# One token list for the order of attention on all engines, k and q evacuated apart, loads by single batches with q first

## The chip, the cores and the metric

The kernel runs on one core of a Trainium2 chip. The metric is the device time of one execution in microseconds (us), as the median of several runs. Each engine of the core (TensorE or PE for matrix products, VectorE or DVE, ScalarE or ACT, GpSimd or POOL, SyncE or SP) works off its own instructions in the order in which the program lists them; semaphores make one wait for another. DMAs that GpSimd, SyncE and ScalarE issue share 16 DMA engines.

## The reference

Two parts, the second fed by the first. Attention over 8 batches, 12 heads, 448 tokens and 64 features, with q and k normalised over the features:

```python
q_n, k_n = (rmsnorm(q, g_q), rmsnorm(k, g_k))      # x / sqrt(mean(x*x) + 1e-6) * g
scores = scale * np.matmul(q_n, k_n.transpose(0, 1, 3, 2))
attn = softmax(scores)
attn_out = np.matmul(attn, v)
```

Then a mixture of eight experts without a learned router. The output of attention, laid out as 3584 tokens by 768, is routed by a hash of each token's id, and a token goes through one expert only:

```python
expert_idx = token_ids * np.int64(2654435761) % np.int64(E)
for e in range(E):
    h = np.maximum(x[mask_e] @ w1[e], 0.0)          # 768 -> 1024
    out[mask_e] = h @ w2[e]                         # 1024 -> 768
```

## The kernel before

**Attention** goes by steps: a step is one pair of heads of one batch, so there are 48 steps, numbered 0 to 47, six to a batch. Steps are gathered in groups that are prepared together: groups 0, 1 and 2 hold the one, two and three head pairs of batch 0, every later group holds three (two groups to a batch, 17 groups in all).

*Preparation of a group*, for q (a = 0) and k (a = 1): `prep_sq` squares (VectorE, in a few cases ScalarE); `prep_sum` adds the squares by 16 products with the identity on TensorE; `prep_red` reduces them on VectorE; `prep_rr` makes the reciprocal root with Ln and Exp on ScalarE; `prep_norm` multiplies (four VectorE instructions); `prep_v` copies v (VectorE).

*A step*: `transposes` does eight transposes on TensorE (four for k, four for q) into one PSUM bank, `ps_qk`, of which there is one, used by the sums too. `transposed` evacuates them on VectorE, k with the gain to `kT`, then q to `qT`. `score` makes the scores in four pieces (TensorE), each into one of three `ps_sc` buffers, and ScalarE writes the exponential of each. `av_part` makes the products with v in three parts (TensorE, one `ps_av` buffer), and after the third part VectorE takes the reciprocal of the row sums and scales into `x_sb`. After a batch's sixth step `store_x` writes the batch to DRAM (SyncE).

The order is a loop over steps written out by hand: scores 1 and 2 of step s, transposes of s + 1 with their evacuation, score 3, two parts of the products of s - 1, score 0 of s + 1, then what three tables (`pre`, `mid`, `post`) hold for the preparation of later groups, with the third part of the products among it.

**Loads.** q, k and v come as float32 from DRAM and are cast to 16 bits on the way by DMAs that GpSimd issues, one after another in its program order (`load_q` two DMAs, `load_kv` four for k and four for v). Only step 0's q and k come by SyncE and ScalarE (float32). Buffers hold two batches each, two of every kind. Before the loop GpSimd issues batch 0 in two parts, batch 1 whole, batches 2 and 3 together; then it clears three gather buffers (L605), the pad slots of the second buffers, and makes constants (`setup2`, L115 to L139). Batches 4 and 5 are loaded together at step 7, 6 and 7 at step 19.

**Routing** (`p1` to `p11`, `table`, `table_mm`) works out which token goes to which slot of which expert. One piece is put into each step from step 14 on, behind that step's other work. Pieces use several engines: `p1` takes the low bits of the ids on VectorE and converts them on GpSimd (`eidf`, L367); `p2` compares on VectorE (`onehot`, L371) and converts the counts on GpSimd (`oc`, L374); `p3` multiplies them with `emask` and ones on TensorE (L382 to L384) and copies the products out on VectorE (`cmix`, L385):

```python
        def p2():
            V.tensor_tensor(out=onehot[:], in0=eidf[:, None, :].to_broadcast([P, E, NTC]), ...)
            V.reduce_sum(ot[:], onehot[:], axis=AX.X)
            G.tensor_copy(oc[:], ot[:])
```

**Experts.** From about step 44 GpSimd gathers tokens from DRAM; the first three tiles are transposed behind the last scores, then for each expert `gemm1` (L766), `gemm2` (L779) and an indirect store (L784). Weights of experts 0 and 1 are loaded during attention, the others afterwards, by GpSimd.

Of the kernel before, what the change touches and what calls it, by code (L numbers as in the profile page):

```python
# [19 lines left out]
def kernel(  # L20
# [12 lines left out]
    nc = tc.nc  # L33
# [70 lines left out]
    def setup():  # L104
        import dataclasses as _dc
        tid_t32 = _dc.replace(moe_token_ids.tensor, shape=[N * 2], dtype=I32)
        for base in (0, D):
            nc.sync.dma_start(out=gcol[base:base + D, 0:1], in_=g_q[:, None])
            nc.sync.dma_start(out=gcol[base:base + D, 1:2], in_=g_k[:, None])
        nc.scalar.dma_start(out=tid32[:],  # L110
                            in_=bass.AP(tensor=tid_t32, offset=0,
                                        ap=[[2 * NTC, P], [2, NTC], [1, 2]]))
# [86 lines left out]
    with tc.manual_schedule(), \  # L199
# [66 lines left out]
        def prep_sq(gi, a, on_act=False):  # L266
# [5 lines left out]
            if on_act:  # L272
# [4 lines left out]
        def prep_sum(gi, a, wide=False):  # L277
# [3 lines left out]
            if wide:  # L281
# [17 lines left out]


        def prep_rr(gi):
            n = groups[gi][2]
            ss = st[gi].pop("ss")
            m = 8 * n
            rr = a_st.tile([P, 2, GMAX * 8, 2], FP16, name="rr")
            nc.scalar.activation(ss[:, :, 0:m], ss[:, :, 0:m], AF.Ln, bias=eps_col[:], scale=1.0 / D)
# [3 lines left out]
            st[gi]["n8"] = a_n8.tile([P, 2, GMAX, 4, 2, D], FP16, name="n8")  # L310

        def prep_norm(gi):
            n = groups[gi][2]
            rr = st[gi].pop("rr")
            n8 = st[gi]["n8"]
            for a in (1, 0):
                f = raw(a, gi).rearrange("p n (hh j) (u t) -> p n hh j u t", hh=2, t=2)
                for hh in range(2):
                    nc.vector.tensor_tensor(
                        out=n8[:, a, 0:n, :, hh, :].rearrange("p n j (u t) -> p n j u t", t=2),  # L320
                        in0=f[:, :, hh],
                        in1=rr[:, a, 4 * n * hh:4 * n * hh + 4 * n].rearrange(
                            "p (n j) t -> p n j t", j=4)[:, :, :, None, :].to_broadcast(
                                [P, n, 4, D // 2, 2]),
                        op=ALU.mult)
# [139 lines left out]
        qkt = {}  # L465
        pend = {}
        xs = {}

        def transposes(s, evac=True):
            gi, i = steps[s]  # L470
            n8 = st[gi]["n8"]
            T32 = ps_qk.tile([P, 512], FP32, name="qkT_ps")
            T = T32[:].bitcast(FP16)
            for a in (1, 0):
                for j in range(4):
                    o = 512 * a + P * j
                    nc.tensor.transpose(T[:, o:o + P], n8[:, a, i, j].rearrange("p h d -> p (h d)"),  # L477
                                        ident16[:])
            qkt[s] = T
            if evac:  # L480
                transposed(s)

        def transposed(s):
            T = qkt[s]
            kT = a_qk.tile([P, 512], FP16, name="kT")
            qT = a_qk.tile([P, S], FP16, name="qT")
            nc.vector.tensor_scalar(out=kT[:], in0=T[:, 512:1024], scalar1=g_col[:], scalar2=None,  # L487
                                    op0=ALU.mult)
            nc.vector.tensor_copy(qT[:], T[:, 0:S])  # L489
            qkt[s] = (qT, kT)  # L490

        def score(s, j):
            qT, kT = qkt[s]
            expT = pend[s][0]
            sc = ps_sc.tile([P, 2, 512], FP32, name="sc_ps")
            if j < 3:
                for hh in range(2):
                    nc.tensor.matmul(sc[:, hh, :S], lhsT=kT[64 * hh:64 * hh + 64, P * j:P * j + P],  # L498
                                     rhs=qT[64 * hh:64 * hh + 64, :], start=True, stop=True)
                nc.scalar.activation(expT[:, 2 * j:2 * j + 2, :], sc[:, :, :S], AF.Exp,  # L500
                                     bias=0.0, scale=1.0)
            else:
                nc.tensor.matmul(sc[:, 0, :S], lhsT=kT[:, 384:512], rhs=qT[:, :],  # L503
                                 start=True, stop=True)
                nc.scalar.activation(expT[:, 6, :], sc[:, 0, :S], AF.Exp, bias=0.0, scale=1.0)  # L505
                qkt.pop(s)

        def av_part(s, part):
            gi, i = steps[s]
            b, hp0, n = groups[gi]  # L510
            hp = hp0 + i
# [4 lines left out]
            expT, av = pend[s]  # L516
# [14 lines left out]
            else:  # L531
# [6 lines left out]
                if b not in xs:  # L538
                    xs[b] = a_x.tile([P, SL, HW], FP16, name="x_sb")
                x_sb = xs[b]  # L540
                srec = a_st.tile([P, SL], FP32, name="srec")
                nc.vector.reciprocal(srec[:], av[:, :, D])
                nc.vector.tensor_tensor(  # L543
                    out=x_sb[:, :, hp * D:hp * D + D], in0=av[:, :, :D],
                    in1=srec[:, :, None].to_broadcast([P, SL, D]), op=ALU.mult)
                pend.pop(s)
                if hp == HP - 1:
                    store_x(b)
# [17 lines left out]
        load_kv([nc.sync, nc.scalar, nc.sync, nc.scalar], first[:, 1], k, 0, 0, 1)  # L566
        load_q([nc.sync, nc.scalar], first[:, 0], 0, 0, 1)
        setup()
        make_identity(nc, ident16[:])
        pool = [nc.gpsimd] * 4  # L570
        load_kv(pool, part_of(k_bufs, 0, 1, 2), k, 0, 1, 2)
# [356 lines left out]
```

## Time and profile before

| what | us |
|---|---|
| median of three runs (378.47 to 381.21) | 379.61 |
| the profiled execution | 374.72 |
| its span | 373.2 |
| busy: PE, DVE, ACT, POOL | 343.4, 216.1, 190.3, 175.6 |
| first exponential of attention (ScalarE) | 13.69 |
| output of step 0, step 14, step 39, step 47 scaled (VectorE, start) | 23.27, 74.72, 160.12, 186.25 |
| first product of the experts in full flow (TensorE) | 185.9 |
| last indirect store issued (GpSimd) | 367.81 |

The page cuts the span into 40 slices of 9.33 us and gives each engine's busy share of a slice in tenths. A query over windows gives busy microseconds and the number of instructions for each engine in stretches that the reader chooses, and the clock granted to TensorE. The timeline lists instructions in order of time: start, length, engine, line, what is written and read, and in brackets the idle time of the engine just before, with what ended it. Start to start is the time that an instruction costs its engine; its length is a little more, since neighbours overlap. A long busy share says only that an engine worked; which wait ends last in a stretch says what a change there is worth.

### The profile page before, as it was taken

The page shows a single profiled execution, that of the slowest core. Times are in us where ns is not written, and L with a number is a line of the kernel's source. Part 1 is how long each engine was busy: PE and PEld are TensorE (multiplying, and loading weights), DVE is VectorE, ACT ScalarE, POOL GpSimd, SP SyncE. Part 2 cuts the span into 40 slices and gives each one's busy share as a digit, 9 for nine tenths or more (in the row PEclk, how much of TensorE's full clock was granted, in tenths as well). Part 3 has the DMA queues.
Part 4 walks back from the last instruction along what each step waited for, and adds up shares of the span by engine and source line. Part 5 has one row for each costly group of instructions (what it writes and reads, how often), then busy time and mean ns, then how long its engine had stood idle before and what let it go on. Part 6 is the DMA issues. An engine that isn't in the chain of part 4 may idle for free. (4 is left out here: it accounts for less than half of the span.)

```text
span 373.2 us, 9220 instructions
## 1 busy us (share of the span) xinstructions
PE 343.4 (92%) x3862; PEld 231.1 (62%) x3862; DVE 216.1 (58%) x514; ACT 190.3 (51%) x288; POOL 175.6 (47%) x247
## 2 busy tenths in 40 slices
PE   7778879999989999999899999999998997999992
PEld 3456656767666666675676766666665664666661
DVE  4578979999999999989443333232232232332311
ACT  4777879999989999999312121211111111111110
POOL 8887981027439930003328335463654645633122
PEclk9999999999999999999899999999999999999997
DMA  8999999927999992274536999999999999972112
GB/s 123 159 192 195 185 221 191 216 40 127 194 211 211 223 217 52 46 162 108 128 93 141 209 238 252 211 261 223 203 254 177 250 219 188 241 259 91 58 42 112
DMA packets 54268, 64.59 MB, mean 173 GB/s; under 512 B 22403, under 2 KB 42134, under 8 KB 53968
## 3 DMA queue, kind: packets, MB, share of 16 engines
q0 software_dynamic: 50592, 57.98, 88.4%
q1 hardware_dynamic: 3024, 5.41, 5.3%
q8 instruction: 31, 0.51, 0.6%
q10 hardware_dynamic: 608, 0.59, 0.5%
q14 instruction: 13, 0.11, 0.1%
HBM read 89.68 MB, written 18.09 MB: 289 GB/s over the span
## 5 line engine op out<-in xcount | busy, mean ns | idle before, releaser
L500 ACT ACTIVATE expT<-sc_ps 128x896 bf16<-128x896 f32 x144 | 125.2, 923 | 10.8 <-PE sc_ps L498 9.8
L779 PE MATMUL o_ps<-w_sb,h_sb 128*128 128x256 f16 (+1 forms) x512 | 87.9, 326 | 0.0
L766 PEld LDWEIGHTS <-w_sb 128*128 128x128 f16 x432 | 58.0, 144 | 26.4 <-issue 2.0
L766 PE MATMUL h_ps<-xT,w_sb 128*128 128x512 f16 x336 | 73.7, 379 | 0.0
L779 PEld LDWEIGHTS <-h_sb 128*128 128x128 f16 x512 | 48.8, 98 | 32.7
L770 ACT ACTIVATE h_sb<-h_ps 128x512 f16<-128x512 f32 (+2 forms) x36 | 19.7, 549 | 77.2 <-PE h_ps L766 77.2
L784 POOL DMA_INDIRECT out_dram<-o_sb,gidx x32 | 32.9, 1029 | 49.0 <-ACT o_sb L783 17.0
L772 DVE TENSOR_SCALAR h_sb<-h_ps 128x512 f16<-128x512 f32 (+2 forms) x36 | 22.8, 632 | 56.3 <-PE h_ps L766 56.3
L173 POOL DMA_INDIRECT xg<-x_scratch,gidx x32 | 32.5, 1016 | 43.1 <-DVE xg L846 16.0
L783 ACT COPY o_sb<-o_ps 128x768 f32<-128x768 f32 x16 | 12.8, 798 | 74.8 <-PE o_ps L779 56.4
L498 PE MATMUL sc_ps<-qT,kT 64*128 64x448 f16 x288 | 44.0, 356 | 3.7 <-DVE qT L489 2.1
L522 PEld LDWEIGHTS <-expT 128*128 128x128 bf16 x864 | 37.0, 98 | 9.8 <-DVE x_sb L543 6.3
L522 PE MATMUL av_ps<-v,expT 128*128 128x65 bf16 x864 | 40.6, 194 | 1.5 <-DVE x_sb L543 1.5
L783 DVE COPY o_sb<-o_ps 128x768 f32<-128x768 f32 x16 | 15.3, 958 | 43.1 <-PE o_ps L779 21.2
L830 POOL DMA_DIRECT2D w_sb<-in_moe_w_dram x36 | 23.1, 648 | 31.2 <-DMA w_sb<-in_moe_w_dram 29.8
L477 PEld LDWEIGHTS <-n 128*128 128x128 f16 x384 | 22.4, 97 | 24.7 <-issue 15.4
L477 PE MATMUL qkT_ps<-ident,n 128*128 128x128 f16 x384 | 30.3, 220 | 6.7 <-DVE ss L298 3.8
L543 DVE TENSOR_TENSOR x_sb<-av_ps,srec 128x448 f16<-128x448 f32 x48 | 29.7, 619 | 1.5
L185 DVE COPY xT<-xT_ps 128x768 f16<-128x768 f16 x28 | 15.5, 554 | 25.3 <-PE xT_ps L184 25.2
L287 PEld LDWEIGHTS <-ident 128*128 128x128 f16 x544 | 23.6, 98 | 9.1 <-issue 6.5
L505 ACT ACTIVATE expT<-sc_ps 128x448 bf16<-128x448 f32 x48 | 26.9, 560 | 1.1 <-PE sc_ps L503 1.1
L487 DVE TENSOR_SCALAR kT<-qkT_ps,g_col 128x512 f16<-128x512 f16 x48 | 23.0, 480 | 4.1 <-PE qkT_ps L477 3.4
(145 smaller groups left out, 422.6 us busy)
## 6 DMA issues: line engine op xcount, KB each, us to landing
w_sb<-in_moe_w_dram POOLq DMA_DIRECT2D x32, 384.0 KB, 13.1
w_sb<-in_moe_w_dram POOLq DMA_DIRECT2D x12, 768.0 KB, 14.1
x_scratch<-x_sb SPq DMA_DIRECT2D x15, 288.0 KB, 5.9
w_sb<-in_moe_w_dram POOLq DMA_DIRECT2D x2, 1536.0 KB, 14.5
kr<-in_k_dram POOLq DMA_DIRECT2D x6, 384.0 KB, 10.2
qr<-in_q_dram POOLq DMA_DIRECT2D x3, 768.0 KB, 14.5
vr<-in_v_dram POOLq DMA_DIRECT2D x6, 384.0 KB, 19.8
kr<-in_k_dram POOLq DMA_DIRECT2D x6, 288.0 KB, 10.0
```

What stands on the lines that cost most here:

```text
L173: nc.gpsimd.indirect_dma_start(out=xg[:], out_offset=None, in_=x_dram[0:rows, :], in_offset=bass.IndirectOffsetOnAxis(ap=idx, axis=0), bou ...
L287: nc.tensor.matmul(sp.rearrange("p (hh n j) w -> p hh n (j w)", hh=2, j=4), lhsT=ident16[:], rhs=sq[:, c, 0:m].rearrange("p (n hh j) w -> ...
L477: nc.tensor.transpose(T[:, o:o + P], n8[:, a, i, j].rearrange("p h d -> p (h d)"), ident16[:])
L498: nc.tensor.matmul(sc[:, hh, :S], lhsT=kT[64 * hh:64 * hh + 64, P * j:P * j + P], rhs=qT[64 * hh:64 * hh + 64, :], start=True, stop=True)
L500: nc.scalar.activation(expT[:, 2 * j:2 * j + 2, :], sc[:, :, :S], AF.Exp, bias=0.0, scale=1.0)
L505: nc.scalar.activation(expT[:, 6, :], sc[:, 0, :S], AF.Exp, bias=0.0, scale=1.0)
L522: nc.tensor.matmul(av[:, 2 * t + hh, :], lhsT=expT[:, tl(hh, j), P * t:P * t + P], rhs=v8[:, i, 4 * hh + j, 0:D + 1], start=(hh == 0 and t ...
L543: nc.vector.tensor_tensor(out=x_sb[:, :, hp * D:hp * D + D], in0=av[:, :, :D], in1=srec[:, :, None].to_broadcast([P, SL, D]), op=ALU.mult)
L766: nc.tensor.matmul(h_ps[:, :c1 - c0], lhsT=w1v[:, co, fo, :], rhs=xT[:, co, c0:c1], start=(co == 0), stop=(co == CO - 1))
L779: nc.tensor.matmul(o_ps[:, d0:d1], lhsT=h_sb[:, fo, col * P:(col + 1) * P], rhs=w2_sb[:, fo, d0:d1], start=(fo == 0), stop=(fo == FO - 1))
L783: (nc.vector.tensor_copy if col % 2 else nc.scalar.copy)(o_sb[:], o_ps[:])
L784: scat = nc.gpsimd.indirect_dma_start(out=out[:, :], out_offset=bass.IndirectOffsetOnAxis(ap=idx, axis=0), in_=o_sb[:], in_offset=None, bo ...
```

## The change

The order of attention is no longer a loop with tables. A list of tokens, each an operation with its step or group, is read from left to right and issued on all engines: one list written out up to step 9, and one for a group of three steps that is repeated for groups 4 to 16. Operations are cut finer: transposes, evacuations, scores, exponentials, row sums and output scaling are separate tokens, q and k apart. What had been done at a step's end (loads, a routing piece, weight loads, gathers) moves to `hooks`, called after the previous step's output. Squares of group 0's k and group 3's k go to ScalarE, those of groups 1 and 2 come back to VectorE. Zeroing before the loop is reordered. Loads go by single batches or halves with q first: on GpSimd q of heads 1 and 2 precedes the identity, batches 0 and 1 come in halves, the second buffers are cleared ahead of batches 2 and 3, these come one after the other, and the constants follow them; batch 4 is loaded at step 6, batch 5 at step 9, batch 6 at step 15, batch 7 at step 21. The gains and the token ids are loaded by three DMAs in place of five.

```diff
+        ACT_SQ = ((0, 1), (3, 1))
+        WIDE_SUM = ((0, 0), (1, 0), (1, 1))
...
-        def transposes(s, evac=True):
+        def transpose(s, a):
...
+            for j in range(4):
+                o = 512 * a + P * j
+                nc.tensor.transpose(T[:, o:o + P], n8[:, a, i, j].rearrange("p h d -> p (h d)"),
+                                    ident16[:])
...
+        def evacuate(s, a):
+            T = qkt[s]
+            if a:
+                kq[s] = (a_qk.tile([P, 512], FP16, name="kT"), a_qk.tile([P, S], FP16, name="qT"))
+                nc.vector.tensor_scalar(out=kq[s][0][:], in0=T[:, 512:1024], scalar1=g_col[:],
+                                        scalar2=None, op0=ALU.mult)
+            else:
+                nc.vector.tensor_copy(kq[s][1][:], T[:, 0:S])
...
+        def put_x(s):
...
+            if hp == HP - 1:
+                store_x(b)
+            hooks(s + 1)
...
-        load_qk(1, 0, HP)
-        load_v(1, 0, HP)
-        load_qk(2, 0, 2 * HP)
-        load_v(2, 0, 2 * HP)
...
+        load_q([nc.sync, nc.scalar], first[:, 0], 0, 0, 1)
+        load_kv([nc.sync, nc.scalar, nc.sync, nc.scalar], first[:, 1], k, 0, 0, 1)
+        setup()
         nc.vector.memset(warm[:], 0.0)
...
+        load(0, 1, 2, "q")
+        make_identity(nc, ident16[:])
+        load(0, 1, 2, "k")
+        load(0, 0, 3, "v")
+        load(0, 3, 3)
+        load(1, 0, 3)
+        load(1, 3, 3)
         zero_kv(nc.gpsimd, k_bufs[1], 0, 2 * HP)
         zero_q(nc.gpsimd, q_bufs[1], 0, 2 * HP)
         zero_kv(nc.gpsimd, v_bufs[1], 0, 2 * HP)
+        load(2, 0, HP)
+        load(3, 0, HP)
+        for xg in xg_e:
+            nc.gpsimd.memset(xg[:], 0.0)
         setup2()
...
-            if hp == 1 and b % 2 and b + 3 < B:
-                load_qk(b + 3, 0, 2 * HP)
-                load_v(b + 3, 0, 2 * HP)
+        def hooks(s):
+            if s >= NS:
+                return
             gi, i = steps[s]
+            b, hp = groups[gi][0], groups[gi][1] + i
+            if s == HP:
+                load(4, 0, HP)
+            if hp == 3 and 1 <= b and b + 4 < B:
+                load(b + 4, 0, HP)
             if side and s >= 14:
                 side.pop(0)()
...
+        steady = """
+            Tk:1 Tq:1 sc:0.1 sc:0.2 av:-1.0 kT:1 av:-1.1 qT:1 exp:0.1 exp:0.2 v:1 sc:0.3 sumq:1
+            sqk:2 redq:1 av:-1.2 sc:1.0 sc:1.1 exp:0.3 ln:1 sc:1.2 er:1 Tk:2 exp:1.0 Tq:2 rec:-1
+            x:-1 av:0.0 nk:1.0 kT:2 qT:2 av:0.1 exp:1.1 sc:1.3 av:0.2 sumk:2 sc:2.0 exp:1.2
+            nk:1.1 sc:2.1 exp:1.3 nq:1.0 sc:2.2 exp:2.0 rec:0 nq:1.1 redk:2 Tk:3 x:0 Tq:3 av:1.0
+            kT:3 exp:2.1 av:1.1 qT:3 sqq:2 sc:2.3 av:1.2 rec:1 sc:3.0 exp:2.2 exp:2.3 x:1 exp:3.0
+        """
+        for g in range(4, NG):
+            emit(steady, g, s0[g])
```

In the list, `Tk` and `Tq` are transposes, `kT` and `qT` evacuations, `sc` and `exp` scores and exponentials, `av` the products with v, `rec` and `x` row sums and output, `sqk` to `nq` the preparation; the number after the colon counts steps (or groups) from the group's first, the one after the dot is the piece. The part of q and of k in a bank, the number of each operation and every tile pool are as before.

## The prediction

> **What bounds the kernel now.** I read the page's slices first, then the stretches by engine, then VectorE's and GpSimd's instructions in order of time. The slices (9.33 us each) of GpSimd's busy share and of the DMA engines:
>
> ```profile
> POOL 8887981027439930003328335463654645633122
> DMA  8999999927999992274536999999999999972112
> ```
>
> Attention fills slices 1 to 20. GpSimd issues loads until the seventh slice, and the DMA engines stay full to the eighth (about 75 us). The stretches (busy us and count per engine, clock, DMA share, GB/s):
>
> ```profile
> 80.00:100.00 20.00, 19.43 (x343) 13.79 (x342) 19.62 (x51) 18.95 (x29) 11.76 (x21) 1.00 0.87 125
> 100.00:120.00 20.00, 18.33 (x323) 12.86 (x319) 19.37 (x52) 18.40 (x29) 12.26 (x18) 1.00 1.50 209
> 120.00:140.00 20.00, 18.92 (x331) 13.20 (x328) 19.80 (x55) 18.64 (x29) 13.75 (x20) 1.00 1.03 219
> 140.00:160.00 20.00, 19.33 (x350) 13.50 (x348) 19.54 (x56) 18.19 (x29) 0.63 (x1) 1.00 0.26 55
> ```
>
> VectorE is busy 78.3 of these 80 us, so a new order can win at most 1.7 us there. A group of three steps takes 9.85 us (kT starts at 140.42 and 150.27, with no idle time shown between). ScalarE needs less for a group: a wide exponential starts every 0.81 us, a narrow one takes 0.43, Ln with the next Exp 0.55, so 9 x 0.81 + 3 x 0.43 + 0.55 = 9.13 us. From 183 us on TensorE is nearly full to the end, so a later end of attention moves the whole end.
>
> Before 60 us there is room: VectorE is busy 44.4 of 60 us, and ScalarE's idle pieces between its first exponential (13.69) and 60 us add up to about 8 us. One of them:
>
> ```profile
> 54.27 0.56 DVE L330 COPY v<-vr 128x1536 bf16<-128x1536 bf16 x1 [2.16 <-DMA vr<-in_v_dram]
> ```
>
> Now GpSimd's own instructions, where each DMA piece stands with its issue time and its wait:
>
> ```profile
> 14.09 1.34 POOL L240 DMA_DIRECT2D kr<-in_k_dram  x2
> 15.87 1.43 POOL L240 DMA_DIRECT2D kr<-in_k_dram  x2 [0.45 <-DMA qr<-in_q_dram]
> 17.94 0.75 POOL L230 DMA_DIRECT2D qr<-in_q_dram  x1 [0.64 <-DMA vr<-in_v_dram]
> ...
> 58.28 0.74 POOL L240 DMA_DIRECT2D vr<-in_v_dram  x1 [1.05 <-DMA kr<-in_k_dram]
> 72.19 0.21 POOL L367 CAST eidf<-eid 128x28 f32<-128x28 int32 x1 [13.17 <-DVE eid L365]
> ...
> 76.14 0.19 POOL L374 CAST oc<-ot 128x8 bf16<-128x8 f32 x1 [3.70 <-DVE ot L373]
> ```
>
> Counted in issue order, the load at 15.87 is the 23rd and is released by the 15th (qr), that at 17.94 the 25th, released by the 17th (vr); the 50th, at 58.28, by the 42nd. So **at most eight GpSimd DMAs are in flight**, and each wait gives a landing time. Call one tensor of one head pair a "pair": 13 had landed by 15.8 us, 34 (batches 0 and 1) by 30.4, 76 by 58.3, 106 (six batches) by 75, where the stretch 70 to 75 us still moves 245 GB/s and the next one 57. That is 93 pairs in 59.2 us, with two batches' output stores among them, **0.637 us a pair**; piecewise 0.70 (13 to 34) and 0.56 (76 to 106). After the loads GpSimd stands idle 13.17 us until VectorE asks for the first routing conversion, at 72.19: routing never waits for GpSimd now.
>
> **The change part by part.**
>
> *Front.* Group 0's k square goes to ScalarE, q loads lead, the steps are interleaved further, v of batch 2 no longer waits behind batch 3's q and k (the 2.16 us above). Of the 8 us of ScalarE idle time I credit half, 4 us, since group 2's loads still land when they do: step 14's output would come at 70.7 us instead of 74.7. Bounds: 0 and 8.
>
> *k and q evacuated apart.* No instruction is added: 48 kT (0.48 us) and 48 qT (0.38) stay. VectorE's work per group is the same 9.85 us with a table pair in each step, and going through the steady list by hand with these durations I find no wait on VectorE. Gain from there on: 0 to 1.7 us, I take 1.2. At the end, the first two parts of step 46's value products come ahead of the transposes of gathered rows (now 181.09 to 182.54 us behind them): 0.8 us, bounds 0 and 1.5.
>
> *Loads.* Before, two batches were loaded by ten DMAs, issued at steps 7 and 19. Now every batch has ten of its own: 0 to 3 ahead of GpSimd's constants, 4 at step 6, 5 at step 9, 6 at step 15, 7 at step 21. GpSimd works in order, and the order of the changed program is: batches 0 and 1, zeros, batches 2 and 3, constants, batches 4 and 5, then `eidf` (routing piece p1, step 14), batch 6, and only then `oc` (p2, step 15). VectorE's `onehot` after step 14's output waits for `eidf`. TensorE's product with `emask` (p3), which stands ahead of the q transposes of step 18, waits for `oc`, and behind it in TensorE's order stand all further scores. This adds two waits:
>
> - Batches 0 and 1: 8 q DMAs at 0.67 us, 32 others at 0.62 (four in 2.51), identity 0.75, from 0.96: 26.9 us.
> - Zeros, 36.56 to 41.33 in the trace: 4.8, so 31.7.
> - Batches 2 and 3, 20 DMAs. The last one goes out when the 12th, 24 pairs on, has landed: the queue has run empty, so 2.1 us (the shortest landing of the trace, 48 KB) + 24 x 0.637 + 0.7 to issue it: 49.8. Issue alone, 4 x 0.75 + 16 x 0.73: 46.4.
> - The three xg zeros and the constants, 2.2 + 6.5: 58.5.
> - Batches 4 and 5 in the same way, +18.1: **`eidf` at 76.6**, where `onehot` is ready at 70.7. VectorE waits about 6 us.
> - Batch 6: its last DMA waits for 42 pairs from 58.5 us: 58.5 + 2.1 + 26.8 + 0.7: **`oc` at 88.1**. From 76.6, `onehot` and the sums (0.7) and the work up to step 15's output (3.9) bring TensorE to the product at 81.3: it waits about 7 us.
>
> Compare with now, the first instruction after p3 and the kT of step 18:
>
> ```profile
> 79.49 0.38 DVE L385 CAST cmix<-sc_ps 112x224 bf16<-112x224 f32 x1
> ...
> 79.96 0.47 DVE L487 TENSOR_SCALAR kT<-qkT_ps,g_col 128x512 f16<-128x512 f16 x1
> ```
>
> With 0.5 us for `oc` and the products this piece starts at 88.6, **9.1 us later than 79.49**. The front's gain is gone in these waits: they end when the DMAs land, whoever was early. Bounds: at 0.56 us a pair `oc` comes at 82.9 (+3.9), at 0.70 at 92.2 (+13.2); with no DMA wait at all, from issue times alone, at 77.4 (-1.6).
>
> *The rule on small transfers* ("DMA: Bandwidth & Descriptors", Measured (HBM→SBUF, 128 partitions, SWDGE, issued from GpSimd)). The 96 KB pieces of v land 4.7 us after issue; with eight in flight that is one each 0.59 us, under the 0.62 us that issuing takes, so I add nothing for the halved sizes. The Trainium skill, on the page named, asks for transfers of at least 1 MiB, and its fit gives each DMA 2 us of fixed time; my estimate from that page is 30 more DMAs x 2 us / 8 in flight, 7.5 us on top by `oc`.
>
> *The clock.* TensorE now idles longer than anywhere in attention. The trace has one such place (busy us, clock):
>
> ```profile
> 179.00:180.00 1.00, 0.39 (x6) 0.38 (x6) 0.56 (x1) 1.00 (x3) 0.70 (x2) 1.00 0.64 177
> 180.00:181.00 1.00, 0.35 (x7) 0.24 (x5) 0.56 (x1) 0.28 (x1) 1.00 (x2) 1.00 0.45 146
> 181.00:182.00 1.00, 1.00 (x21) 1.00 (x19) 0.56 (x1) 0.00 (x0) 0.18 (x1) 0.54 0.69 194
> 182.00:183.00 1.00, 1.00 (x18) 0.79 (x17) 0.00 (x0) 0.00 (x0) 0.00 (x0) 0.50 0.97 142
> 183.00:184.00 1.00, 1.00 (x4) 0.56 (x5) 0.83 (x2) 0.00 (x0) 0.00 (x0) 0.50 1.11 180
> 184.00:185.00 1.00, 1.00 (x11) 0.62 (x10) 0.00 (x0) 0.00 (x0) 0.00 (x0) 0.76 0.32 55
> ```
>
> After 3 us at under half load the clock is at 0.50 to 0.54 for 3 us. TensorE has about 1 us of slack in a group, so a cold stretch after each wait costs 0 to 1.7 us; I take 0.5.
>
> **Sum.** +9.1 - 1.2 - 0.8 + 0.5 = +7.6 us on the profiled execution's 374.72 us, 382.3. The median of the runs shown is 379.61, 4.9 above that execution, so on their scale **387.2 us**.
>
> **Rivals.**
>
> 1. *GpSimd is in time* (the other side). If loads land faster than any stretch shows, only issue time counts: `oc` at 77.4, -1.6 there, and -2.0 later: 376.0 us, at best 374.8. It decides from `oc` before about 79.5. For it: now GpSimd waits 13 us for work there. Against it: by then 112 pairs must have landed, which takes 78.8 us at 0.637 from 15.8 on with no gap, and the change puts three gaps in the stream (issuing in small pieces, zeros, constants).
> 2. *The order adds waits of its own* in the stretch where VectorE is full, say 0.3 us (such as its 0.39 us wait at 106.52) in each of 13 groups: +4, 391 us. Against it: the hand pass.
> 3. *Halved DMAs move less.* From 5 to 15 us, with the smallest pieces, the stretches move 141 and 146 GB/s, later 191 to 200. At three quarters of the rate a pair costs 0.85 us and `oc` comes at 102: +23.1 - 1.5, 401.2 us. Against it: in those 10 us GpSimd issues without a wait, so issuing sets the rate there.
>
> That the change doesn't do what it says: in the VectorE-full stretch a better order has nothing to win; this is in the forecast.
>
> **How the numbers follow.** Chances: forecast 0.74, in time 0.12, own waits 0.09, slow DMAs 0.05. The forecast's bounds are +0.7 (`oc` at 82.9 with all later gains, 3.9 - 1.7 - 1.5) to +14.9 (at 92.2 with none and the full cold cost, 13.2 + 1.7). About 1% (3.8 us) is what these runs, 378.47 to 381.21, can tell from no change. Of the forecast 0.10 lies within it; half of the first rival is faster by more. Faster 0.06, same 0.16, slower 0.78. The range 378.5 to 394 leaves out most of rival 1 (0.11), all of 3 and the last microsecond of the forecast, about 0.2 in all.
>
> **What would show it.** Right: GpSimd busy or waiting for DMAs without a break until after 80 us, VectorE idle before `onehot` with GpSimd as releaser, TensorE idle several us before the `emask` product, and kT of step 18 at 85 to 92 us; a group of 9.8 to 9.9 us after that. The front: step 5's output before 44.1 us. Wrong: `eidf` issued without a wait, or idle VectorE inside the table steps, or attention ending at another distance from `oc` than now (about 107 us from 79.5 to 186.8).

## The result and the profile after

| us | before | after |
|---|---|---|
| median, side by side on one chip | 379.04 (377.75 to 381.21) | 397.11 (394.69 to 399.14) |
| ratio, 95% interval | | **1.0468 (1.039 to 1.0546)** |
| profiled execution; its span | 374.72; 373.2 | 399.14; 397.6 |
| output of step 14 scaled (VectorE, start) | 74.72 | 75.60 |
| `eidf`, `oc` (GpSimd, start) | 72.19, 76.14 | 83.86, 94.57 |
| first `cmix` copy (VectorE, start) | 79.49 | 95.06 |
| output of step 47 scaled | 186.25 | 210.52 |

The kernel is slower, as forecast, but by 18.1 us of median where 7.6 were forecast; 397.1 lies outside the range. The two profiled executions lie 24.4 us apart. In every ratio, here and below, executions more than 1.5% above the fastest of their kernel are left out.

The page's slices of GpSimd and of the DMA engines, of the changed kernel (9.94 us each):

```profile
POOL 8998668564455990000601834446265454642111
DMA  8997998999499892246333699999999999992112
```

GpSimd now issues loads until the tenth slice, and the DMA engines dip in the fourth and the seventh, where the row of before had only nines from its second to its eighth slice.

GpSimd's timeline, each DMA or conversion with the wait before it:

```profile
33.31 0.77 POOL L231 DMA_DIRECT2D qr<-in_q_dram  x1
...
52.88 0.64 POOL L241 DMA_DIRECT2D vr<-in_v_dram  x1 [1.88 <-DMA qr<-in_q_dram]
53.52 2.11 POOL L652 MEMSET xg<- 128x768 f16 x3
...
61.91 0.82 POOL L231 DMA_DIRECT2D qr<-in_q_dram  x1
...
83.22 0.64 POOL L241 DMA_DIRECT2D vr<-in_v_dram  x1 [0.95 <-DMA qr<-in_q_dram]
83.86 0.22 POOL L369 CAST eidf<-eid 128x28 f32<-128x28 int32 x1
...
94.57 0.20 POOL L376 CAST oc<-ot 128x8 bf16<-128x8 f32 x1
```

In these rows neither conversion waits for its input any more (before, 13.17 and 3.70 us): GpSimd comes to them late, behind its DMAs. What waits is shown by the list of waits from 76 to 100 us (engine, tile and line, what was waited for: total, times, longest):

```profile
PE qkT_ps L291 <- DVE qT L491: 8.5, 1, 8.5
DVE onehot L373 <- POOL ones_e L370: 7.9, 1, 7.9
DVE cmix L387 <- PE sc_ps L385: 6.6, 1, 6.6
...
PE sc_ps L384 <- POOL oc L376: 5.4, 1, 5.4
```

Those are the two waits of the forecast, VectorE at `onehot` (7.9 us, forecast 6) and TensorE at the `emask` product (5.4, forecast 7). In the timeline of VectorE the piece ends here:

```profile
95.06 0.39 DVE L387 CAST cmix<-sc_ps 112x224 bf16<-112x224 f32 x1 [6.63 <-PE sc_ps L385]
...
95.54 0.47 DVE L488 TENSOR_SCALAR kT<-qkT_ps,g_col 128x512 f16<-128x512 f16 x1
```

`cmix` is 15.57 us later than before, kT of step 18 comes at 95.54 instead of 79.96. The stretches, in the columns of before (busy us and count of PE, PEld, DVE, ACT, POOL, clock, DMA share, GB/s):

```profile
80.00:100.00 20.00, 8.51 (x83) 5.52 (x84) 8.39 (x24) 4.50 (x6) 10.72 (x22) 0.50 1.46 185
100.00:120.00 20.00, 19.59 (x350) 14.09 (x348) 18.59 (x47) 18.86 (x29) 10.22 (x18) 0.99 1.03 149
120.00:140.00 20.00, 18.66 (x327) 12.86 (x325) 19.44 (x56) 18.54 (x29) 16.36 (x22) 1.00 0.89 185
140.00:160.00 20.00, 19.33 (x342) 13.45 (x338) 19.86 (x57) 19.03 (x30) 8.88 (x13) 1.00 0.59 116
```

The loss stands in the first row: VectorE is busy 8.4 of 20 us, and the clock is 0.50 for all of it. Afterwards VectorE is full again, in groups of three steps that take 9.6 to 9.7 us (kT starts at 143.62, 153.33 and 162.93).

### The profile page after: what moved, and what is told of

It reads as the page before. It is cut to its first block, busy times and chain, and to the rows that moved or that the text cites. A ratio compares the mean times of both kernels' runs of the same rounds, so it can differ in the third digit from the quotient of the medians.

```text
span 397.6 us, 9220 instructions
## 1 busy us (share of the span) xinstructions
PE 347.2 (87%) x3841; PEld 235.7 (59%) x3841; DVE 214.9 (54%) x515; ACT 187.6 (47%) x285; POOL 198.3 (50%) x287
## 5 line engine op out<-in xcount | busy, mean ns | idle before, releaser
L517 ACT ACTIVATE expT<-sc_ps 128x896 bf16<-128x896 f32 x144 | 122.4, 935 | 19.8 <-PE sc_ps L499 17.2
L174 POOL DMA_INDIRECT xg<-x_scratch,gidx x32 | 32.6, 1019 | 50.1 <-DVE h_sb L784 17.3
L796 POOL DMA_INDIRECT out_dram<-o_sb,gidx x32 | 32.9, 1028 | 49.5 <-ACT o_sb L795 17.4
L795 ACT COPY o_sb<-o_ps 128x768 f32<-128x768 f32 x16 | 12.8, 798 | 74.2 <-PE o_ps L791 52.5
L499 PE MATMUL sc_ps<-qT,kT 64*128 64x448 f16 x288 | 43.0, 371 | 4.8 <-issue 2.3
L534 PE MATMUL av_ps<-v,expT 128*128 128x65 bf16 x864 | 43.3, 199 | 4.2 <-DVE x_sb L563 3.5
L534 PEld LDWEIGHTS <-expT 128*128 128x128 bf16 x864 | 39.1, 101 | 13.2 <-DVE x_sb L563 10.1
L291 PEld LDWEIGHTS <-ident 128*128 128x128 f16 x544 | 26.6, 103 | 22.9 <-DVE qT L491 17.5
L481 PE MATMUL qkT_ps<-ident,n 128*128 128x128 f16 x384 | 32.7, 229 | 3.8 <-DVE kT L488 1.6
L481 PEld LDWEIGHTS <-n 128*128 128x128 f16 x384 | 24.1, 102 | 17.0 <-issue 12.6
L520 ACT ACTIVATE expT<-sc_ps 128x448 bf16<-128x448 f32 x48 | 27.7, 576 | 13.4 <-PE sc_ps L502 11.3
L241 POOL DMA_DIRECT2D vr<-in_v_dram x40 | 25.8, 660 | 14.3 <-DMA qr<-in_q_dram 13.6
L186 DVE COPY xT<-xT_ps 128x768 f16<-128x768 f16 x28 | 15.5, 553 | 26.1 <-PE xT_ps L185 22.2
```

The source lines that it names most:

```text
L174: nc.gpsimd.indirect_dma_start(out=xg[:], out_offset=None, in_=x_dram[0:rows, :], in_offset=bass.IndirectOffsetOnAxis(ap=idx, axis=0), bou ...
L291: nc.tensor.matmul(sp.rearrange("p (hh n j) w -> p hh n (j w)", hh=2, j=4), lhsT=ident16[:], rhs=sq[:, c, 0:m].rearrange("p (n hh j) w -> ...
L534: nc.tensor.matmul(av[:, 2 * t + hh, :], lhsT=expT[:, tl(hh, j), P * t:P * t + P], rhs=v8[:, i, 4 * hh + j, 0:D + 1], start=(hh == 0 and t ...
L795: (nc.vector.tensor_copy if col % 2 else nc.scalar.copy)(o_sb[:], o_ps[:])
L796: scat = nc.gpsimd.indirect_dma_start(out=out[:, :], out_offset=bass.IndirectOffsetOnAxis(ap=idx, axis=0), in_=o_sb[:], in_offset=None, bo ...
```

## The experiments

They ran on several chips, whose medians of the kernel before lie between 372.65 and 380.04 us; each is told as its ratio to the kernel before on its own chip, and each profile is read by the starts of the steps' outputs on VectorE.

**1. Is it routing behind the loads? `vec_routing`.**

```diff
         def p1():
-            G.tensor_copy(eidf[:], eid[:])
-            G.memset(ones_e[:], 1.0)
+            V.tensor_copy(eidf[:], eid[:])
+            V.memset(ones_e[:], 1.0)
...
         def p2():
-            G.tensor_copy(oc[:], ot[:])
+            V.tensor_copy(oc[:], ot[:])
```

(and the six instructions of p4 likewise)

> The changed kernel, with the GpSimd instructions of routing pieces p1 to p4 (two conversions, a memset, five small ones and one more conversion) on VectorE; the loads stay as they are. Theory A (the loss is routing standing behind the loads in GpSimd's order): no engine waits for GpSimd at p2 and p3, the first cmix copy starts at about 80 us instead of 95.06, and the time falls by about 15 us less 1 us for eight small VectorE instructions, to 381 to 384 us. Theory B (the loads themselves are late: their data is what attention lacks): the wait moves to the squares or v copies of batches 4 to 6 and the time stays above 392 us. Theory C (the new order costs time in every group and at the end of attention): some 8 us of the 18 remain, 388 us or more.

Measured: ratio **1.0074** (1.0031 to 1.0116), on the scale of 379.04 us 381.8. VectorE's timeline:

```profile
75.33 0.38 DVE L373 TENSOR_TENSOR onehot<-eidf,iota_f 128x224 bf16<-128x224 f32 x1
...
80.06 0.39 DVE L387 CAST cmix<-sc_ps 112x224 bf16<-112x224 f32 x1 [0.40 <-PE sc_ps L385]
```

Theory A holds: with the same loads, both waits are gone and with them 0.039 of the 0.047. Theory B falls: no square or v copy of batches 4 to 6 takes their place. Theory C falls too: its 388 us would be a ratio of 1.024.

**2. Do the two waits add? `eid_vec`**, p1's two lines of the edit above alone.

> The changed kernel with only p1's two GpSimd instructions (the conversion eidf and a memset) on VectorE; p2's conversion oc stays on GpSimd behind the loads of batch 6. Theory A says that the two waits stand in series but that the end is set by the second alone: onehot starts without a wait at about 76 us, TensorE then waits some 12 to 13 us instead of 5.4 for oc, cmix still starts at 94 to 95 us, and the time is 395 to 398 us. The rival (each wait costs its own length, 6.9 and 6.6 us): about 390 us.

Measured: ratio 1.0468 (1.0375 to 1.0562), to the last digit that of the full change. `onehot` starts at 75.46 without a wait, and the time comes back in one piece (VectorE's timeline):

```profile
94.43 0.39 DVE L387 CAST cmix<-sc_ps 112x224 bf16<-112x224 f32 x1 [14.84 <-PE sc_ps L385]
```

The first wait costs nothing by itself; when `oc` comes alone sets the loss. The rival's 390 us would be a ratio of 1.029, below the interval.

**3. The two halves of the change: `order_alone` and `loads_alone`.** The first is the changed kernel with the loads of before, the second the kernel before with the changed loads.

```diff
+        load(2, 0, 2 * HP, "kqv")
         zero_kv(nc.gpsimd, k_bufs[1], 0, 2 * HP)
...
-        load(2, 0, HP)
-        load(3, 0, HP)
...
-            if s == HP:
-                load(4, 0, HP)
-            if hp == 3 and 1 <= b and b + 4 < B:
-                load(b + 4, 0, HP)
+            if hp == 1 and b % 2 and b + 3 < B:
+                load(b + 3, 0, 2 * HP, "kqv")
```

That is the core of `order_alone`, which also loads batches 0 and 1 in the old order (k first); `loads_alone` makes the opposite edit in the kernel before.

> The token list and all else of the changed kernel, with the loads, zeros and constants on GpSimd in the order and sizes of the kernel before (batches 2 and 3 by ten DMAs ahead of the zeros and constants; 4 and 5 by ten at step 7, 6 and 7 by ten at step 19). Theory A: GpSimd is free when routing starts, cmix starts near 79 us, the time is 377 to 382 us. Theory C (the order itself costs time): 386 us or more.

> The kernel before, with its own order, and the loads, zeros and constants of the changed kernel (q first, halves and single batches, zeros ahead of batches 2 and 3, constants behind them, 4 to 7 at steps 6, 9, 15, 21). Theory A: the waits at onehot and at the emask product come here too, cmix starts at 93 to 96 us, the time is 393 to 397 us. Rival (the loads harm only together with the new order): 379 to 384 us.

Measured: order alone 1.0038 (0.9988 to 1.0088), loads alone **1.0513** (1.042 to 1.0607). In the old order VectorE waits 7.99 us at `onehot` and 6.37 at `cmix`, which starts at 93.78. The loads make the loss in either order; the new order alone makes no difference that can be told. It does not win either: VectorE's first outputs come at 27.99 us (step 0, before 23.27), since the list wants q first and these loads bring k first, and at step 8 VectorE waits 3.60 us for v of batch 2, before 2.16. Its `cmix` comes at 83.26 us, not near 79.

**4. Why are the loads late? `double_23`.** The stretches of the changed kernel around GpSimd's zeros (28.6 to 33.3 us) and constants (53.5 to 61.9):

```profile
30.00:32.00 2.00, 1.87 (x42) 1.49 (x40) 1.94 (x5) 1.60 (x3) 1.95 (x3) 1.00 0.25 34
32.00:34.00 2.00, 2.00 (x36) 1.32 (x32) 1.97 (x7) 1.93 (x4) 1.95 (x3) 1.00 0.00 0
34.00:36.00 2.00, 1.99 (x33) 1.37 (x33) 1.99 (x7) 2.00 (x4) 2.00 (x4) 1.00 0.51 47
36.00:38.00 2.00, 1.43 (x30) 1.21 (x31) 1.50 (x4) 2.00 (x4) 2.00 (x5) 1.00 1.45 194
...
58.00:60.00 2.00, 2.00 (x48) 1.64 (x48) 2.00 (x6) 2.00 (x3) 1.74 (x8) 1.00 0.80 101
60.00:62.00 2.00, 1.93 (x33) 1.30 (x33) 1.66 (x6) 2.00 (x4) 1.78 (x8) 1.00 0.02 2
62.00:64.00 2.00, 2.00 (x31) 1.04 (x27) 1.97 (x6) 2.00 (x4) 2.00 (x3) 1.00 0.23 23
64.00:66.00 2.00, 1.98 (x48) 1.73 (x46) 2.00 (x6) 2.00 (x4) 2.00 (x4) 1.00 1.14 146
```

Twice the stream runs empty for some 5 us (last column). In flow it moves 191 to 196 GB/s, 0.59 us for a pair of 114.7 KB (448 tokens x 64 x 2 heads x 2 bytes). The eight DMAs in flight when GpSimd turns to the zeros belong to a half batch and hold 6 pairs, 3.5 us; those ahead of the constants hold 12 pairs, 7 us, and are partly done by then. The zeros take 4.7 us, the xg zeros with the constants 8.4, and the first data come some 2 us after the next issue.

```diff
-        load(2, 0, HP)
-        load(3, 0, HP)
+        load(2, 0, 2 * HP)
```

> The changed kernel with batches 2 and 3 loaded together by ten DMAs in place of twenty; all else stays, so routing still stands behind the loads. Theory G (the stream of loads is not slow, it runs empty: eight single-batch DMAs in flight are too little to bridge the constants): no stretch without data at 59 to 64 us, oc comes 5 to 6 us earlier than 94.57 (88 to 90), and the ratio to the kernel before falls from 1.047 to 1.03 to 1.035. Rival S (the smaller DMAs move less per us while they run): the rate in full flow, 191 to 196 GB/s, rises, the empty stretch stays. Rival B (batches 5 and 6 wait for their buffers, not for the stream): oc stays within 2 us of 94.6 and the time within 1%.

Measured: ratio 1.0293 (1.024 to 1.0346), `oc` at 89.80. The second gap is gone:

```profile
58.00:60.00 2.00, 2.00 (x30) 1.19 (x30) 0.99 (x3) 1.43 (x2) 0.64 (x1) 0.92 1.61 210
60.00:62.00 2.00, 2.00 (x43) 1.43 (x39) 1.97 (x5) 2.00 (x4) 0.64 (x1) 1.00 1.07 313
62.00:64.00 2.00, 1.97 (x42) 1.53 (x38) 2.00 (x5) 2.00 (x4) 0.00 (x0) 1.00 1.49 203
```

Theory G holds (the ratio just under its range), and S falls: from 38 to 58 us, with DMAs of twice the size, the rate is 178 to 196 GB/s, not higher. Rival B falls too, since `oc` comes 4.8 us earlier although attention itself is later (step 14's output at 83.26 us). But the way to the end is another: all twelve pairs of q come first now, and VectorE waits for the k of batch 2:

```profile
53.23 0.96 DVE L279 TENSOR_TENSOR sq_k<-kr 128x1536 f16<-128x1536 f16 x1 [12.55 <-DMA kr<-in_k_dram]
```

This wait of 12.6 us at step 5 stands ahead of the routing waits and hides most of them (`cmix` waits 2.35 us).

**5. Where did the front's gain go? `zeros_behind_2`.** The changed kernel has this wait too, smaller:

```profile
44.61 0.96 DVE L279 TENSOR_TENSOR sq_k<-kr 128x1536 f16<-128x1536 f16 x1 [3.70 <-DMA kr<-in_k_dram]
```

Both orders square the k of batch 2 between the outputs of steps 4 and 5. Before, its DMAs are issued from 22.29 us on, ahead of the zeros; the change issues the zeros first, then q, then this k, from 34.80 us on. In `zeros_behind_2` routing p1 to p5 is on VectorE and

```diff
+        load(2, 0, HP)
         zero_kv(nc.gpsimd, k_bufs[1], 0, 2 * HP)
         zero_q(nc.gpsimd, q_bufs[1], 0, 2 * HP)
         zero_kv(nc.gpsimd, v_bufs[1], 0, 2 * HP)
-        load(2, 0, HP)
```

> The kernel of run vec_routing, with p5's four small instructions on VectorE too, and with GpSimd's zeros of the second buffers issued behind the load of batch 2 instead of ahead of it. If the front lost its gain to the k of batch 2 (VectorE idle 2.62 us there in vec_routing), step 5's output comes at 42.5 to 43.5 us instead of 45.40, step 14's at 72 to 73.5 instead of 74.79; and the 1.61 us that VectorE waits at `over` (step 20) goes. Together 2.5 to 4 us: a ratio to the kernel before of 0.997 to 1.001 where vec_routing has 1.0074. Rival: the front is bound by loads that land at their rate whatever the order; step 14 stays at 74 to 75 us, ratio 1.003.

Measured: ratio 0.9991 (0.9952 to 1.0031). Step 5's output comes at 42.93, step 14's at **69.78**, 5.0 us earlier than in `vec_routing` (twice what I had expected) and 4.9 earlier than before. Profiles with the same loads spread: step 14's output comes at 73.18 to 77.13 us in the six with the loads of the changed kernel (`after`, `after_again`, `late_gather`, `eid_vec`, `vec_routing`, `vec_again`), at 68.63 to 71.57 in the five with batch 2 ahead of the zeros (this run and, below, `spins`, `table_41`, `hl_vec`, `route_13`). The two sets do not overlap, and their means are 5.0 us apart. Not all of it reaches the end; the profile names where it goes, the same queue once more:

```profile
111.37 0.43 DVE L446 TENSOR_SCALAR w_sb<-iota_h,hl 128x128 f16<-128x128 f16 x2 [4.55 <-POOL hl L443]
```

Attention is now early enough to ask for p11's conversion `hl` while GpSimd is still busy with the DMAs of expert 0's weights.

**6. The clock: `spins`.** In the first profile of the changed kernel the clock is 0.50 from 10 to 22 us, before it is 1.00. This run adds idle products to `zeros_behind_2`:

```diff
-            sqq:0 zero:3 spin:9 sumq:0 sqk:0 sumk:0 spin:3 redq:0
+            sqq:0 zero:3 spin:9 sumq:0 spin:5 sqk:0 sumk:0 spin:3 redq:0
...
```

> The same, with eleven more idle products (spin) on TensorE in the first 13 us: 5 behind the first q sums, 5 in place of 1 behind group 1's q sums, 2 in place of 1 behind its k sums, 1 behind step 0's transposes. If the clock of 0.50 from 8 to 22 us costs time in the front, it stays at 1.00 and step 0's output comes 0.7 to 1.5 us earlier than 23.7, and some of it reaches step 14 (ratio down by 0.001 to 0.003). Rival: TensorE has slack in the front, step 4's output stays within 0.3 us and the ratio does not change.

Measured: ratio 1.0111 (1.0076 to 1.0145). The clock is 1.00 from 6 to 22 us and step 0's output comes 0.6 us earlier, but step 4's comes 2.0 later: VectorE waits 2.72 and 3.10 us for k pieces (17.88 and 32.00). But the spins are not what decides about the clock: `after_again`, the changed kernel itself (run 10), has 1.00 from 8 to 22 us, and so has `hl_vec` (run 8), without spins. What goes with a cold clock can be read from profiles with the same instructions up to step 5. In `after`, `eid_vec`, `vec_routing` and `vec_again` it is 0.51 to 0.52 from 8 to 22 us, in `after_again` and `late_gather` 1.00: step 0's output comes at 23.69 to 23.88 us against 20.35 and 20.69, step 4's at 39.52 to 39.73 against 38.33 and 39.06, step 5's at 45.40 to 46.40 against 45.36 and 46.33. So the cold clock goes with some 3 us at step 0 (whether it causes them is not shown), and at step 5, behind the wait for batch 2's k, nothing of that is left. Why the run is 1.2% slower is not settled (in the two profiles 1.8 us stand at step 14's output and 2.3 in the still stand of run 10); the spins alone do not explain it, since `table_41`, below, has them too.

**7. A wait of the order's own: `table_41`.** From step 38's output to step 39's the changed kernel takes 6.16 us, the kernel before 4.68. The last routing piece stands there, and in the new order VectorE idles 1.94 us at it, before 0.19 (VectorE's timeline, before and after):

```profile
156.25 0.22 DVE L456 TENSOR_SCALAR emp<-sc_ps 128x64 f32<-128x64 f32 x1 [0.19 <-PE sc_ps L452]
```

```profile
173.75 0.22 DVE L458 TENSOR_SCALAR emp<-sc_ps 128x64 f32<-128x64 f32 x1 [1.94 <-PE sc_ps L454]
```

The edit, on top of `spins`:

```diff
-            if side and s >= 14:
+            if side and s >= (14 if len(side) > 1 else 41):
```

> The same, with the last routing piece (28 products and four VectorE instructions) two steps later, behind the group's last output instead of the group's first. With the new order this step pair (38 to 39) takes 6.15 us, with the old one 4.68. If the place in the group costs that, the pair takes 3.4 us and the step that now holds the piece 4.5 to 5: 1 to 1.7 us less, ratio down by 0.003 to 0.004. Rival: the piece costs 2.8 us wherever it stands, no change.

Measured: ratio 0.9951 (0.9917 to 0.9984). Steps 38 to 41 take 10.04 us instead of 11.71 in `spins`: the place did cost 1.7 us. The ratio falls by 0.016 against `spins`, far more than the 0.003 to 0.004 expected, and by 0.004 against `zeros_behind_2`; the first includes what was not settled in `spins`, so the 1.7 us rest on the profiles.

**8. Two ways to a better kernel: `pairs_of_batches` and `hl_vec`.** Both have the edit of run 7 and no spins. The first is the changed kernel with the loads of `order_alone` from batch 2 on, routing on GpSimd; the second is `zeros_behind_2` with

```diff
-            G.tensor_copy(hl[:], parts[:])
+            V.tensor_copy(hl[:], parts[:])
```

> The changed kernel with its start (batches 0 and 1, q first) kept, but from batch 2 on the loads of the kernel before: batches 2 and 3 together, k first, ahead of the zeros and constants; 4 and 5 together at step 7, 6 and 7 at step 19. Routing stays on GpSimd; the last routing piece stands two steps later, as in table_41. Theory (the backlog of double loads covers the constants, k first meets the early square): no wait at onehot, at the emask product or at the k square of batch 2, cmix at 75 to 78 us, a ratio to the kernel before of 0.985 to 0.997. Rival (the front is bound by the rate of the loads; nothing of the new order's gain reaches the end): 1.000 to 1.005.

> The kernel of run zeros_behind_2 (without the spins of the next two runs), with the last routing piece two steps later, as in table_41, and with the conversion hl of piece p11 on VectorE. In zeros_behind_2 VectorE waits 4.55 us for hl, which stands on GpSimd behind the loads of expert 0's weights. If that wait is on the path, step 25 takes about 4.3 us instead of 7.3 and the ratio to the kernel before is 0.985 to 0.990 (table_41 has 0.9951); if the wait only moves to the next piece on GpSimd, it stays at 0.993 to 0.999. For the spins: if they cost time, as run spins against zeros_behind_2 suggests (1.0111 against 0.9991), this run gains more than the hl wait, below 0.985; if they do not, the rest is as said.

Measured: 1.0193 (1.0139 to 1.0246) and 1.0019 (0.9979 to 1.0059). Both miss, each by a transfer that something earlier had covered. In the first `onehot` does not wait, as expected, but `cmix` comes at 85.10 us: the double load puts v of batch 2 behind twelve pairs each of k and q, and the list, which is early, waits for it:

```profile
58.33 0.56 DVE L332 COPY v<-vr 128x1536 bf16<-128x1536 bf16 x1 [6.75 <-DMA vr<-in_v_dram]
```

In the second the `hl` wait is gone (step 24 to 25 in 2.65 us instead of 7.30) and step 45's output comes at 173.63, 4.0 us earlier than before; then TensorE waits for the gathered rows:

```profile
178.00 0.76 PE L185 MATMUL qkT_ps<-ident,xg 128*128 128x128 f16 x6 [2.66 <-DMA xg<-x_scratch,gidx]
```

The load of expert 1's second weight (1.5 MB) waits for the last routing piece, which I had moved two steps back. It goes out at 159.2 us, and the store of batch 6 (162.6 us), for which the gathers wait, takes 9.9 us beside it; in `vec_routing` 3.4. The lists of DMAs show it (the store's two large ones, last number: us from issue to landing), `hl_vec` and then `vec_routing`:

```profile
x_scratch<-x_sb SPq DMA_DIRECT2D x2, 288.0 KB, 9.9
```

```profile
x_scratch<-x_sb SPq DMA_DIRECT2D x2, 288.0 KB, 3.4
```

`table_41` and `pairs_of_batches`, with the same move of the piece, have 9.8 and 9.7 us, so this is a second cause for the miss of the latter.

**9. The piece earlier instead of later: `route_13` and `k_first`.**

```diff
-            if side and s >= (14 if len(side) > 1 else 41):
+            if side and s >= 13:
```

This is `route_13`, on top of `hl_vec`; `k_first` adds `"kqv"` to the loads of batch 0's second half and of batches 1 and 2.

> The kernel of run hl_vec with all routing pieces one step earlier (from step 13), so that the last one stands at the end of a group as there, but three steps before it (38, not 41). In hl_vec the load of expert 1's second weight (1.5 MB), which waits for that piece, is issued at 159.2 us, and the store of batch 6's output (162.6 us) takes 9.9 us beside it instead of 3.4 to 4.4; the gathers start 12.9 us after step 41's output instead of 7 to 8, and TensorE waits 2.66 us for them. Theory (that collision eats the gain): the store takes 4 to 6 us, the gathers start 7 to 9 us after step 41's output, and the ratio to the kernel before is 0.990 to 0.996 where hl_vec has 1.0019. Rival (the stall of about 2 us on TensorE, VectorE and ScalarE during the gathers, seen in zeros_behind_2 and spins, comes back and takes the place): 1.000 to 1.004.

> The same, with k loaded ahead of q for heads 3 to 5 of batch 0 and for batches 1 and 2, since the token list squares k first in these groups. In hl_vec VectorE waits 1.80 us for k at 29.21 and 1.98 us at 41.22. Theory: the first wait goes, step 3's output comes 1 to 2 us earlier, of which at most 1 us reaches the end: ratio 0.988 to 0.995, 0.001 to 0.003 under route_13. Rival (q is squared right behind k, so its landing sets the step whichever is first): no difference within 0.001.

Measured: `route_13` **0.987** (0.9818 to 0.9923), 375.0 us against 379.93 beside it: the version that beats the kernel before most clearly so far (the interval of `table_41` ends just below 1). The store takes 3.4 us. The rival's still stand comes back too (6.07 us from step 44 to 45), and the ratio is lower than both had it. `k_first` 0.982 (0.9756 to 0.9884), from three of its six executions (370.79 to 375.64 us): the two intervals overlap, and in its profile step 3's output comes only 0.2 us earlier than in `route_13`, so whether k first adds anything is open.

**10. The end of attention: `after_again`, `vec_again`, `late_gather`.** In the first profile of the changed kernel TensorE, VectorE and ScalarE stand still after step 44's output, while GpSimd issues the first gathers. ScalarE's timeline there, and the same instructions in `after_again`:

```profile
196.54 0.54 ACT L520 ACTIVATE expT<-sc_ps 128x448 bf16<-128x448 f32 x1 [2.15 <-remote]
199.52 2.54 ACT L517 ACTIVATE expT<-sc_ps 128x896 bf16<-128x896 f32 x3 [2.43 <-remote]
```

```profile
193.69 0.70 ACT L520 ACTIVATE expT<-sc_ps 128x448 bf16<-128x448 f32 x1
194.12 2.71 ACT L517 ACTIVATE expT<-sc_ps 128x896 bf16<-128x896 f32 x3
```

`after_again` and `vec_again` are the two kernels unchanged; `late_gather` is the changed kernel with

```diff
-            if s == NS - 4:
+            if s == NS - 2:
                 for kt in range(KT - 1):
                     gather(xg_e[kt], gidx[:, kt:kt + 1], N_EARLY)
```

> The changed kernel as it is, beside vec_again. From step 44's output to step 45's the profile of the changed kernel shows 8.42 us, that of vec_routing 3.13. If the still stand belongs to the kernel (its order or where its instructions lie), it comes again here, 6 to 8.5 us, and not in vec_again; if it belongs to the chip, both have it or neither has. The ratio to the kernel before 1.042 to 1.052.

> The kernel of run vec_routing as it is, beside after_again. Belongs to the kernel: step 44 to 45 in 3.1 us again, ratio 1.003 to 1.011. Belongs to the chip: as after_again has it; with it, 6 to 8 us there and a ratio of 1.01 to 1.02.

> The changed kernel with the first three gathers and what follows them on GpSimd issued behind step 45's output, two steps later. If the still stand comes with the gathers, step 44 to 45 takes 3.1 us and the stand comes later or not at all; TensorE then waits for the gathered rows ahead of step 46's third part, and the end of attention is no earlier than in after_again. If it comes with the place in the program, step 44 to 45 takes 6 to 8.5 us as in after_again.

Measured: ratios 1.0427 (1.0375 to 1.0478), 1.007 (1.0016 to 1.0123) and 1.0385 (1.0329 to 1.044). Step 44 to 45 takes 3.1 us in all three; the stand does not come. So it does not belong to the kernel alone: one profile of it has the stand (8.4 us), the next has not. It shows in the profiles of `zeros_behind_2`, `spins`, `double_23`, `route_13` and `k_first` too (6.0 to 8.4 us), which come from two chips, and in none from the chips of runs 1 to 3 and of these three. `table_41`, on one of those two chips, has 3.13 us there; its first gather starts at 179.37 us, behind step 45's output, as in the two runs of 8. `late_gather` could not tell more: there was no stand to move, and the edit hardly moved the gathers, since GpSimd does not wait for VectorE's outputs (the first starts 8.1 us after step 41's output instead of 6.3, still ahead of step 44's). What it is stays open.

## Why the prediction was right in sign and short in size

`after_again` gives the account without the stand: `cmix` is 15.5 us later than before, and step 47's output too (201.72 against 186.25). The terms, by the prediction's own steps:

- **Loads: +9.1 forecast, +15.6 measured** (+15.5 in `after_again`). This term failed, by its size alone: the mechanism (GpSimd in order, `eidf` behind batch 5, `oc` behind batch 6, and `oc` alone setting the end) is what runs 1 to 3 show. `oc` was forecast for 88.1 and came at 94.57, and kT of step 18 at 95.54, behind the 85 to 92 us named as the sign. Batches 0 and 1 took 1.7 us more, batches 2 and 3 2.1 more, batches 4 and 5 3.9 more; zeros and constants together 0.4 less, batch 6 0.8 less. The step that failed is "24 x 0.637" after an empty queue. 0.637 us was an average over a stream that never ran dry, with two output stores in 93 pairs. Here each stretch of 24 pairs held most or all of a store (0.69 MB), and when the 12th DMA had landed, the ones behind it were partly done as well. The queues of GpSimd's DMAs (q0) and of the stores (q1; packets, MB, share) show it from 33.31 to 52.88 us and from 61.91 to 83.22:

```profile
q0 software_dynamic: 6931, 3.02, 123.3%
q1 hardware_dynamic: 153, 0.59, 8.0%
```

```profile
q0 software_dynamic: 7152, 3.10, 118.2%
q1 hardware_dynamic: 320, 0.69, 9.5%
```

3.02 and 3.10 MB are 26.3 and 27.0 pairs. At 0.195 MB a us, with the 2.1 us of dead time, all these bytes take 20.6 and 21.5 us; measured are 19.6 and 21.3, forecast were 17.4. The bound that was to cover this, 0.70 us a pair, gave 92.2, since it stretched the rate and kept the count. With 15.6 in the sum the forecast would have been 393.7, inside the range; the ratio of `after_again` is 395.2 us on the scale of 379.04, still a little outside it.
- **Front: 4 us forecast at step 14's output, -0.9 measured** (+1.5 in `after_again`). The sign named for it, step 5's output before 44.1 us, did not come (46.40). The order does have the gain: 4.9 us in `zeros_behind_2`. I had assumed that "group 2's loads still land when they do" and looked no further: the next load that this stretch asks for, batch 2's k, had been moved behind the zeros and their gap. For the time it made no difference, as the prediction says: `oc` comes at 94.49 us with step 14 ready at 73.18 (`after_again`) and at 94.57 with 75.60.
- **Order: -1.2 forecast.** Steps 20 to 38 take 58.8 us instead of 60.3, -1.5. Rival 2's mechanism then takes it back, once and not in each group: +1.5 at the last routing piece (run 7).
- **End of attention: -0.8 forecast, -1.3 measured** in `after_again` (step 39 to 47, 24.8 instead of 26.1). The first profile has +7.0 there, with the stand.
- **Clock: +0.5 forecast.** From `cmix` to step 20's output 17.3 us (17.0 in `after_again`) instead of 15.7, +1.3 to +1.6, within its bound of 1.7. The clock is 0.50 from 81 to 100 us; that all of the 1.3 is the clock's was not tried. The rows in the prediction show two microseconds under half load (179 to 181 us), not three.
- **Rival 1** (GpSimd in time) falls with `oc`. **Rival 3** (halved DMAs move less) falls too: 191 to 196 GB/s in flow, with double ones 178 to 196 (run 4). The 7.5 us estimated from the Trainium skill's page "DMA: Bandwidth & Descriptors" (Anatomy of one DMA, a fixed 2 us for each DMA) would have brought `oc` to 95.6, close to the 94.57 measured, but not for its reason: in flow these DMAs move no less than the double ones, and run 4 brought `oc` 4.8 us forward by closing a gap, without a higher rate.

The sum of `after_again` is +15.5 + 1.3 - 1.5 + 1.5 - 1.3 = +15.5 us at step 47, and its median stands 15.7 above that of the kernel before beside it. The first pair of medians differs by 18.1. If that chip has the stand in most executions, as its profile has, the 2 to 3 us more are explained; that is argued, not shown.

## What to carry to other kernels

An engine that issues loads in program order is a queue: a small instruction behind them, on which another engine waits, gets their landing times, so put such instructions on an engine that has no DMAs ahead of them, or ahead of the loads. When the number of DMAs in flight is fixed, smaller DMAs are also a smaller backlog: what the issuing engine does between two loads must be shorter than the backlog, or the stream runs dry, and each restart has to be counted in bytes (dead time, what else shares the stream, what is half done), not by an average rate from a full stream. And each wait that is taken away brings the next cover into view, here in turn k of batch 2, `hl`, and a store beside a weight load: look for what will be asked for earlier before moving anything.

## What the runs showed of the hardware

- Two kernels, `eid_vec` and the full change, differ by a wait of 7.9 us on VectorE and both have the ratio 1.0468: a wait that was followed by a longer one on the same queue cost nothing.
- A store of 0.69 MB took 9.7 to 9.9 us where a weight load of 1.5 MB had been issued 3.4 us ahead of it (`hl_vec`, `table_41`, `pairs_of_batches`), and 3.3 to 4.4 us where the load was 9.5 to 12.8 us ahead (`zeros_behind_2`, `vec_routing`, the kernel before, `route_13`).
- While the first gathers are issued, TensorE, VectorE and ScalarE can stand still for 2 to 6 us with no releaser in the profile; the same kernel shows it in one profile and not in another (8.42 and 3.14 us from step 44 to 45).
- The changed kernel had a TensorE clock of 0.51 from 8 to 22 us in one profile and of 1.00 in another, and its first output at 23.88 and 20.69 us; at step 5 (46.40 and 45.36 us) little was left of that.
